# Counting products of a routing step: float32r operands in place of bfloat16

## Chip, cores and metric

One Trainium2 chip, one of its cores. The metric is the device time of one execution in microseconds (us): three runs of the kernel before gave 1186.3, 1187.3 and 1188.73 us, median 1187.3 us.

## What is computed

Three layers in a row, all with float32 inputs and a float32 output: an attention with normalised queries and keys (4 batches, 12 heads, 448 positions, head size 64), an MLP from 768 to 2048 and back to 768 with a hard-swish between, and a layer of 8 experts. The last assigns each of the 1792 tokens to one expert, and every expert takes at most 224 tokens:

```python
logits = x @ w_gate                          # 1792 x 8
order = np.argsort(-logits.flatten())
for idx in order:
    tok, e = idx // E, idx % E
    if assigned[tok] >= 0 or counts[e] >= cap: continue
    assigned[tok] = e; counts[e] += 1
...
h = np.maximum(x[mask] @ w1[e], 0.0); out[mask] = h @ w2[e]
```

Pairs of token and expert are thus visited from the largest logit down; a token goes to the first expert that still has room.

## The kernel before

The program is one stream per engine. The large products run on TensorE in the type float32r: the operands are split into a high and a low float32r part, and three products (high by high, high by low, low by high) make one.

The attention and the first half of the MLP fill the first 650 us or so. From there to about 890 us TensorE computes the second half of the MLP, `y`, in a loop over tiles of 128 tokens (`passes`, lines 1151 to 1186). For each of 16 slices of the hidden width (`f`) the function `y_mm` (line 1110) is called for three products and two parts of the output, 512 columns (`hf` 0) and 256 columns (`hf` 1). So the products alternate, 512 columns, 256 columns, each with a stationary operand of 128 columns of `g2h` or `g2l`. These operands come by DMA (`gr`), are rounded on ScalarE (line 1053) and get their low part on GpSimd (line 1055).

The routing is done beside this. Its logits `L` are ready before. It is a generator, `routing()` (line 810), that does its work on VectorE and a few small products on TensorE, and yields a number: `y_mm` counts the products of `y`, and when that many have been issued it lets the generator go on (lines 1119 and 1120). The table `Y` (line 62) holds these numbers. They alone set where the routing's small products stand in TensorE's order.

Seven rounds (`r`, line 891) each find, for every expert, the limit above which its tokens are taken:

- `best()` (line 879) marks in `A` (128 partitions x 14 x 8, 0 or 1) the best expert that each token has left.
- Six steps search the threshold digit by digit, three on the high half of the logit's bits (`kh`), three on the low half (`kl`). A step compares all keys with 40 candidates at once, `C` (128 x 14 x 40, 0 or 1, line 917). Then 14 products on TensorE (line 922) count for each candidate and expert: the stationary operand is a slice of `C`, 128 x 40, the moving one a slice of `A`, 128 x 8. VectorE compares the counts with the room left, `G` (40 x 8, line 924). One more product (line 927), with `ones` (40 x 128) stationary, sums `G` over the 40 candidates onto all partitions. VectorE makes of it the next digit (`js`, `pre`, `thr`) and the next `C`.
- The step's yields are `Y[1]` = 11 products of `y` between `C` and its counts and `Y[2]` = 3 between the counts and the product with `ones`.
- At the end of a round three more products: `ones` by `rgb` (line 944), `ones` by `Tb` and `tri` by `Tb` (lines 965 and 966), with `ones` and `tri` 128 x 128 stationary and 14 or 16 moving columns.

After the rounds one product with `tri` (line 998) and 14 with `oh` (line 1017) give the table of tokens, `sidx`, from which the experts' inputs are gathered.

So there are 7 x 6 = 42 bursts of 14 counting products (588), 42 products with `ones` behind them, 7 x 3 at the ends of rounds, and one at line 998. All of these operands are bfloat16 before; `oh` and `mq` (line 1017) are bfloat16 before and after.

```python
if queue: ...
elif cnt[0] >= cnt[1]:                       # y_mm, line 1119
    cnt[1] = cnt[0] + next(route, 10 ** 9)
...
for c in range(NTC):                         # routing, line 921
    nc.tensor.matmul(n, C[:, c, :], A[:, c, :], start=(c == 0), stop=(c == NTC - 1))
```

Of the kernel before, what the change touches and what calls it, by code (L numbers as in the profile page):

```python
# [8 lines left out]
F32 = mybir.dt.float32  # L9
F32R = mybir.dt.float32r  # L10
BF16 = mybir.dt.bfloat16
# [10 lines left out]
def kernel(  # L22
# [14 lines left out]
    nc = tc.nc  # L37
    B, H, S, D = q.shape
    DM, FF = w_in.shape
    E = w_gate.shape[1]  # L40
# [8 lines left out]
    NTC = NT // 128  # L49
# [760 lines left out]
    def routing():  # L810
# [4 lines left out]
        JM = 40  # L815
        V = nc.vector

        def t_(shape, name, dt=F32, bufs=1):
            return rp.tile(shape, dt, name=name, bufs=bufs)

        def psum(p, n):
            return ps.tile([128, 512], F32, name="rt", tag="b", bufs=8)[:p, :n]

        tri = t_([128, 128], "tri", BF16)
        V.tensor_scalar(tri, jp[:, :128], 0.0, None, op0=OP.is_gt)
        ones = t_([128, 128], "ones", BF16)
        V.memset(ones, 1.0)
        ji = t_([128, JM], "ji", I32)
        nc.gpsimd.iota(ji, pattern=[[1, JM]], base=1, channel_multiplier=0)
        jt = {}  # L830
# [42 lines left out]
        def bc(x):  # L873
            return x[:, :, None].to_broadcast([128, NTC, E])

        def be(x):
            return x[:, None, :].to_broadcast([128, NTC, E])

        def best():
            m = t_([128, NTC], "m")  # L880
            V.tensor_reduce(m, Lw, axis=AX.X, op=OP.max)
            w = t_([128, NTC, E], "w")
            V.tensor_tensor(w, Lw, bc(m), op=OP.is_equal)
            V.tensor_tensor(w, w, be(e8), op=OP.mult)
            V.tensor_reduce(m, w, axis=AX.X, op=OP.max)
            A = t_([128, NTC, E], "A", BF16)
            V.tensor_tensor(A, w, bc(m), op=OP.is_equal)
            return A

        yield Y[0]  # L890
        for r in range(E - 1):
            A = best()
            w = t_([128, NTC, E], "w")
            kh = t_([128, NTC], "kh")
            kl = t_([128, NTC], "kl")
            V.tensor_tensor(w, A, hi, op=OP.mult)
            V.tensor_reduce(kh, w, axis=AX.X, op=OP.add)
            V.tensor_tensor(w, A, lo, op=OP.mult)
            V.tensor_reduce(kl, w, axis=AX.X, op=OP.add)
            V.tensor_tensor(kh, kh, U, op=OP.mult)  # L900
            found = []
            for key, (J, steps) in zip((kh, kl), DIG):
                if key is kl:
                    hs = found[0]
                    t = t_([128, NTC], "t16")
                    V.scalar_tensor_tensor(kl, kh, hs, kl, op0=OP.is_equal, op1=OP.mult)
                    V.tensor_scalar(t, kh, hs, 70000.0, op0=OP.is_gt, op1=OP.mult)
                    V.tensor_tensor(kl, kl, t, op=OP.add)
                p = t_([128, 1], "pre" + ("h" if key is kh else "l"))
                V.memset(p, 0.0)  # L910
                for i, x in enumerate(steps):
                    thr = jt[x][:, :J]
                    if i:
                        thr = t_([128, JM], "thr")[:, :J]
                        V.tensor_scalar(thr, jt[x][:, :J], p, None, op0=OP.add)
                    C = t_([128, NTC, JM], "C", BF16)[:, :, :J]
                    V.tensor_tensor(C, key[:, :, None].to_broadcast([128, NTC, J]),  # L917
                                    thr[:, None, :].to_broadcast([128, NTC, J]), op=OP.is_ge)
                    yield Y[1]
                    n = psum(J, E)  # L920
                    for c in range(NTC):
                        nc.tensor.matmul(n, C[:, c, :], A[:, c, :], start=(c == 0), stop=(c == NTC - 1))  # L922
                    G = t_([JM, E], "G", BF16)[:J]
                    V.tensor_tensor(G, n, cap[:J], op=OP.is_ge)
                    yield Y[2]
                    n = psum(128, E)
                    nc.tensor.matmul(n, ones[:J, :], G, start=True, stop=True)
                    js = t_([128, 1], "js")
                    V.tensor_reduce(js, n, axis=AX.X, op=OP.max)
                    V.scalar_tensor_tensor(p, js, float(x), p, op0=OP.mult, op1=OP.add)  # L930
                found.append(p)
            gt = t_([128, NTC], "gt")
            ge = t_([128, NTC], "ge")
            V.tensor_scalar(gt, kl, found[1], None, op0=OP.is_gt)
            V.tensor_scalar(ge, kl, found[1], None, op0=OP.is_ge)
            rg = t_([128, 2, E], "rg")
            for i, x in enumerate((gt, ge)):
                V.tensor_tensor(w, A, bc(x), op=OP.mult)
                V.tensor_reduce(rg[:, i], w.rearrange("p c e -> p e c"), axis=AX.X, op=OP.add)
            rgb = t_([128, 2, E], "rgb", BF16)  # L940
            V.tensor_copy(rgb, rg)
            yield Y[3]
            n = psum(128, 2 * E)
            nc.tensor.matmul(n, ones, rgb.rearrange("p a e -> p (a e)"), start=True, stop=True)
            es = t_([128, E], "es")
            m1 = t_([128, 1], "m1")
            V.tensor_tensor(es, n[:, E:], cap, op=OP.is_ge)
            V.tensor_tensor(es, es, e8, op=OP.mult)
            V.tensor_reduce(m1, es, axis=AX.X, op=OP.max)
            V.tensor_scalar(es, es, m1, None, op0=OP.is_equal)  # L950
            V.tensor_tensor(cap, cap, n[:, :E], op=OP.subtract)
            rem = t_([128, 1], "rem")
            t8 = t_([128, E], "t8")
            V.tensor_tensor(t8, es, cap, op=OP.mult)
            V.tensor_reduce(rem, t8, axis=AX.X, op=OP.add)
            V.tensor_tensor(w, A, be(es), op=OP.mult)
            T = t_([128, NTC], "T")
            V.tensor_reduce(T, w, axis=AX.X, op=OP.add)
            V.tensor_tensor(ge, ge, gt, op=OP.subtract)
            V.tensor_tensor(T, T, ge, op=OP.mult)  # L960
            Tb = t_([128, NTC], "Tb", BF16)
            V.tensor_copy(Tb, T)
            yield Y[4]
            n, n2 = psum(128, NTC), psum(128, NTC)
            nc.tensor.matmul(n2, ones, Tb, start=True, stop=True)
            nc.tensor.matmul(n, tri, Tb, start=True, stop=True)
            cc = t_([128, NTC, NTC], "cc")
            V.tensor_tensor(cc, ctri, n2[:, None, :].to_broadcast([128, NTC, NTC]), op=OP.mult)
            cum = t_([128, NTC], "cum")
            V.tensor_reduce(cum, cc, axis=AX.X, op=OP.add)  # L970
            V.scalar_tensor_tensor(cum, n, rem, cum, op0=OP.subtract, op1=OP.is_lt)
            V.tensor_tensor(T, T, cum, op=OP.mult)
            V.tensor_tensor(gt, gt, T, op=OP.add)
            V.tensor_tensor(U, U, gt, op=OP.subtract)
            V.tensor_tensor(w, A, bc(gt), op=OP.mult)
            V.tensor_tensor(asg, asg, w, op=OP.add)
            V.scalar_tensor_tensor(cap, es, 9999.0, cap, op0=OP.mult, op1=OP.add)
            V.scalar_tensor_tensor(Lw, be(es), -3.0e38, Lw, op0=OP.mult, op1=OP.add)
            yield Y[5]
        A = best()  # L980
        w = t_([128, NTC, E], "w")
        V.tensor_tensor(w, A, bc(U), op=OP.mult)
        V.tensor_tensor(asg, asg, w, op=OP.add)
# [5 lines left out]
        for d in (1, 2, 4, 8):  # L989
# [1 line left out]
            V.tensor_tensor(s2[:, d:], s[:, d:], s[:, :NTC - d], op=OP.add)  # L991
            V.tensor_copy(s2[:, :d], s[:, :d])
            s = s2
        tot = t_([128, E], "tot", BF16)
        V.tensor_copy(tot, s[:, NTC - 1])
        yield Y[6]
        n = psum(128, E)
# [17 lines left out]
        n = psum(CP, 4 * E)  # L1015
# [4 lines left out]
        V.scalar_tensor_tensor(sidx, n[:, :2 * E], 128.0, lo, op0=OP.mult, op1=OP.add)  # L1020

    route = routing()
    SEGS = []
    for t in range(NTC):
# [283 lines left out]
```

## Time and profile before

| what | before |
|---|---|
| median of three runs | 1187.3 us |
| the profiled execution's own time | 1187.51 us |
| its span, first to last instruction | 1185.7 us |
| busy: TensorE products (PE) | 1121.4 us, 95% of the span |
| busy: weight loads (PEld, beside PE) | 907.1 us, 76% |
| busy: VectorE (DVE) | 704.5 us, 59% |
| busy: ScalarE (ACT) | 520.7 us, 44% |
| busy: GpSimd (POOL) | 486.7 us, 41% |
| mean granted TensorE clock | 0.985 of 2.4 GHz |

The time around the span, 1.8 us, is that of start and end. A product shows in the trace as two records, the load of its stationary operand (LDWEIGHTS, PEld) and the product itself (MATMUL, PE). Products are pipelined: a record of a product reaches from its issue to its modelled end, and the next one begins long before that. What a product costs is therefore the distance from its start to the start of the next, and where a product's own load is late, its record begins with the load and is longer by it. In the trace all 4-byte products are called "f32", float32r ones too. A shape such as "128*40 128x8" is contracted rows * stationary columns, and the moving operand.

### The profile page before, as it was taken

The numbers are of one execution on the slowest core, as the hardware profiler recorded it, in microseconds if no ns is written. First come the engines' busy times: TensorE is split into PE (matmuls) and PEld (weight loads), VectorE is DVE, ScalarE is ACT, GpSimd is POOL, SyncE is SP. The second block draws the span as 40 slices with busy tenths as digits, with TensorE's granted clock in tenths as the row PEclk, the third lists the DMA queues.
The fourth block names the chain that finished last, engine by engine and source line by source line (L and its number), as shares of the span: only waits on it lengthen the run. The fifth ranks groups of instructions, "written<-read, shape, count | busy, mean of one in ns | idle before, by whom it ended". The sixth has DMA issues, their size and how long they took to land.

```text
span 1185.7 us, 19464 instructions
## 1 busy us (share of the span) xinstructions
PE 1121.4 (95%) x7204; PEld 907.1 (76%) x7204; DVE 704.5 (59%) x1467; ACT 520.7 (44%) x941; POOL 486.7 (41%) x363
## 2 busy tenths in 40 slices
PE   3888989999999999999999999999997999999997
PEld 2777756667667667787777777777877899999997
DVE  7887877776657744212341566666674756655550
ACT  3655655645545555543442111111123666665550
POOL 2321454664345433112444222222244677765550
PEclk9988999999999999999999999999999999999999
DMA  4465898977776896659986222222235898877731
GB/s 124 116 178 143 248 312 241 314 252 274 236 250 227 267 299 207 213 191 282 354 299 194 69 59 82 59 67 77 63 102 138 252 264 252 232 232 222 234 122 44
DMA packets 210706, 230.83 MB, mean 195 GB/s; under 512 B 24338, under 2 KB 183732, under 8 KB 210612
## 3 DMA queue, kind: packets, MB, share of 16 engines
q1 hardware_dynamic: 207284, 218.58, 59.8%
q0 software_dynamic: 3328, 11.01, 3.1%
q8 instruction: 56, 0.92, 0.3%
q14 instruction: 38, 0.31, 0.1%
HBM read 178.57 MB, written 50.98 MB: 194 GB/s over the span
## 4 chain that ended last, share of the span: by engine, by line
PE 67%; DVE 13%; DMA 8%; issue 5%; ACT 3%; POOL 3%; SPq 1%; POOLq 0%; DVEq 0%; ACTq 0%
PE y L1112 17%; PE h L522 15%; PE y L1260 8%; PE h L1196 5%; PE st L333 4%; PE av L422 3%; PE h L1198 3%; PE av L373 2%; PE sm L431 2%; DMA w<-cv 2%; PE rt L922 2%; DMA we_s<-in_moe_w_dram 1%; DVE C L917 1%; DMA w_hl<-w 1%; PE lg L564 1%
## 5 line engine op out<-in xcount | busy, mean ns | idle before, releaser
L522 PE MATMUL h<-xh,w 128*128 128x448 f32 x768 | 238.5, 380 | 0.8 <-DVE mx L314 0.4
L522 PEld LDWEIGHTS h<-xh,w 128*128 128x128 f32 x768 | 142.9, 190 | 34.8 <-issue 22.2
L1055 POOL TENSOR_TENSOR g2l<-gr,g2h 128x512 fp32r<-128x512 f32 x60 | 78.6, 1311 | 197.3 <-ACT g2h L1053 161.9
L522 PE MATMUL h<-xl,w 128*128 128x448 f32 x384 | 145.4, 379 | 0.0
L314 DVE TENSOR_REDUCE mx<-s 112x1 f32<-112x448 f32 x192 | 105.7, 612 | 51.6 <-PE s L311 51.5
L1053 ACT ACTIVATE g2h<-gr 128x512 fp32r<-128x512 f32 x60 | 37.9, 631 | 222.1 <-PE y L1112 163.9
L1112 PE MATMUL y<-woh,g2l 128*128 128x512 f32 (+1 forms) x448 | 127.8, 347 | 1.0 <-POOL g2l L1055 1.0
L1112 PE MATMUL y<-woh,g2h 128*128 128x512 f32 (+1 forms) x448 | 127.1, 347 | 0.0
L1112 PE MATMUL y<-wol,g2h 128*128 128x512 f32 (+1 forms) x448 | 125.8, 345 | 0.0
L118 POOL TENSOR_TENSOR wel<-we_s,weh 128x768 fp32r<-128x768 f32 x48 | 97.8, 2042 | 40.3 <-ACT weh L117 28.9
L117 ACT ACTIVATE weh<-we_s 128x768 fp32r<-128x768 f32 x107 | 88.4, 841 | 54.1 <-DMA we_s<-in_moe_w_dram 35.8
L118 DVE TENSOR_TENSOR wel<-we_s,weh 128x768 fp32r<-128x768 f32 x59 | 80.0, 1365 | 54.0 <-ACT weh L117 53.8
L344 ACT ACTIVATE ph<-st 112x448 f32<-112x448 f32 x192 | 93.0, 544 | 41.9 <-PE st L333 41.0
L415 POOL TENSOR_TENSOR pa<-ph 112x448 f32<-112x448 f32 x68 | 84.7, 1265 | 47.9 <-ACT ph L344 47.9
L1196 PE MATMUL h<-xe,weh 128*128 128x448 f32 x318 | 101.0, 377 | 1.1 <-DVE xe L1147 1.1
L522 PEld LDWEIGHTS h<-xl,w 128*128 128x128 f32 x384 | 73.1, 190 | 11.4 <-issue 7.1
L1112 PEld LDWEIGHTS y<-woh,g2h 128*128 128x128 f32 x448 | 71.9, 189 | 11.7 <-issue 2.3
L1112 PEld LDWEIGHTS y<-woh,g2l 128*128 128x128 f32 x448 | 72.1, 188 | 10.9 <-POOL g2l L1055 1.3
L1112 PEld LDWEIGHTS y<-wol,g2h 128*128 128x128 f32 x448 | 71.7, 188 | 9.9 <-issue 0.7
L1198 PE MATMUL h<-xe,wel 128*128 128x224 f32 x318 | 76.5, 268 | 0.0
L525 ACT ACTIVATE r<-h,half 128x448 f32<-128x448 f32 x64 | 40.7, 635 | 74.3 <-PE h L522 61.4
L1260 PE MATMUL y<-weh,hh 128*112 128x384 f32 x216 | 73.1, 338 | 0.0
(242 smaller groups left out, 2326.2 us busy)
## 6 DMA issues: line engine op xcount, KB each, us to landing
we_s<-in_moe_w_dram SPq DMA_DIRECT2D x128, 384.0 KB, 3.9
w<-w_hl SPq DMA_DIRECT2D x32, 768.0 KB, 5.7
gr<-g_dr SPq DMA_DIRECT2D x52, 256.0 KB, 2.9
wraw<-in_moe_w_in_dram SPq DMA_DIRECT2D x16, 768.0 KB, 6.8
win_v<-w SPq DMA_DIRECT2D x32, 384.0 KB, 8.2
w_hl<-w SPq DMA_DIRECT2D x16, 768.0 KB, 6.0
wraw<-in_moe_w_out_dram SPq DMA_DIRECT2D x16, 768.0 KB, 5.3
g_dr<-g SPq DMA_DIRECT2D x48, 224.0 KB, 5.0
```

The source lines that it names most:

```text
L117: nc.scalar.activation(hi, raw, AF.Copy)
L118: eng.tensor_tensor(lo, raw, hi.bitcast(F32), op=OP.subtract)
L314: mx = nc.vector.tensor_reduce(MX[i][:, s, c:c + 1], pp[s][:CP, :S], axis=AX.X, op=OP.max)
L333: nc.tensor.matmul(pp[s][:CP, :S], a[r], b[r], start=(n == 0), stop=(n == len(todo) - 1))
L344: nc.scalar.activation(e, pp[s][:CP, :S], AF.Exp)
L415: nc.gpsimd.tensor_tensor(PA[i, s, n], PP[i, s, 2 * n][0], PP[i, s, 2 * n + 1][0], op=OP.add)
L522: nc.tensor.matmul(p[:, :S], lhs[:, c], x[:, c], start=(n == 0), stop=(n == 3 * NC - 1))
L1055: eng.tensor_tensor(gl, g, gh.bitcast(F32), op=OP.subtract)
L1112: nc.tensor.matmul(pp[hf][:, :COLS[hf].stop - COLS[hf].start], a[:, f % QF], w[:, COLS[hf]], start=(f == 0 and n == 0), stop=(f == NF - 1 ...
L1196: mm = [lambda: nc.tensor.matmul(p[:, :4 * CP], wh[:, fo], x.rearrange("d k t -> d (k t)"), start=(c == 0), stop=(c == NC - 1), skip_group ...
L1198: lambda: nc.tensor.matmul(p[:, :2 * CP], wl[:, fo], x[:, 0], start=False, stop=False, skip_group_check=True)]
L1260: nc.tensor.matmul(p[:CP, :HW], a[:, f, tk], w[:, o], start=(f == 0 and n == 0), stop=(f == FB - 1 and n == 2))
```

## The change

All operands of the routing's products but `oh` and `mq` become float32r: `tri`, `ones`, `A`, `C`, `G`, `rgb`, `Tb` and `tot`. VectorE reads `A` through a float32 view. Shapes, counts, the table `Y` and the rest of the program are the same.

```diff
-        tri = t_([128, 128], "tri", BF16)
+        tri = t_([128, 128], "tri", F32R)
         V.tensor_scalar(tri, jp[:, :128], 0.0, None, op0=OP.is_gt)
-        ones = t_([128, 128], "ones", BF16)
-        V.memset(ones, 1.0)
+        ones = t_([128, 128], "ones", F32R)
+        V.memset(ones.bitcast(F32), 1.0)
...
-            A = t_([128, NTC, E], "A", BF16)
+            A = t_([128, NTC, E], "A", F32R)
             V.tensor_tensor(A, w, bc(m), op=OP.is_equal)
-            return A
+            return A, A.bitcast(F32)
...
-            A = best()
+            AR, A = best()
...
-                    C = t_([128, NTC, JM], "C", BF16)[:, :, :J]
+                    C = t_([128, NTC, JM], "C", F32R)[:, :, :J]
...
-                        nc.tensor.matmul(n, C[:, c, :], A[:, c, :], start=(c == 0), stop=(c == NTC - 1))
-                    G = t_([JM, E], "G", BF16)[:J]
+                        nc.tensor.matmul(n, C[:, c, :], AR[:, c, :], start=(c == 0), stop=(c == NTC - 1))
+                    G = t_([JM, E], "G", F32R)[:J]
...
-            rgb = t_([128, 2, E], "rgb", BF16)
+            rgb = t_([128, 2, E], "rgb", F32R)
...
-            Tb = t_([128, NTC], "Tb", BF16)
+            Tb = t_([128, NTC], "Tb", F32R)
...
-        A = best()
+        A = best()[1]
...
-        tot = t_([128, E], "tot", BF16)
+        tot = t_([128, E], "tot", F32R)
```

No instruction of VectorE, ScalarE, GpSimd or the DMA queues changes its place. On TensorE a bfloat16 product is written as two instructions, a load and a product, a float32r one as a single instruction that holds its load. Around the first burst and the product with `ones` behind it, TensorE's order before ends so (the last two counting products, three products of `y`, the load and the product with `ones`, the next of `y`):

```order
L922 LDWEIGHTS C
L922 MATMUL rt<-A,C 40x8
L1112 MATMUL y<-woh,g2h 128x256
L1112 MATMUL y<-wol,g2h 128x512
L1112 MATMUL y<-wol,g2h 128x256
L927 LDWEIGHTS ones
L927 MATMUL rt<-G,ones 128x8 [waits DVE_49]
L1112 MATMUL y<-woh,g2l 128x512 [waits Pool_49]
```

The load of `ones` waits for nothing there; only its product waits for `G`. With the change the same place is:

```order
L922 MATMUL rt<-A,C 40x8 [waits DVE_49]
L922 MATMUL rt<-A,C 40x8 x13
L1112 MATMUL y<-woh,g2h 128x256
L1112 MATMUL y<-wol,g2h 128x512
L1112 MATMUL y<-wol,g2h 128x256
L927 MATMUL rt<-G,ones 128x8 [waits DVE_49]
L1112 MATMUL y<-woh,g2l 128x512 [waits Pool_49]
```

The products stand where they stood; the wait for `G` now holds the load as well. At the end of a round, the same for `Tb`; before:

```order
L965 LDWEIGHTS ones
L965 MATMUL rt<-Tb,ones 128x14 [waits DVE_49]
L966 LDWEIGHTS tri
L966 MATMUL rt<-Tb,tri 128x14
```

and with the change:

```order
L965 MATMUL rt<-Tb,ones 128x14 [waits DVE_49]
L966 MATMUL rt<-Tb,tri 128x14
```

Here too the load of `ones` comes behind the wait.

## Rows read from the trace of the kernel before

**Rows 1.** Busy time by engine, 650 to 890 us: PE, PEld, DVE, ACT, POOL.

```profile
650.00:890.00 240.00, 234.25 (x1719) 186.31 (x1717) 156.83 (x536) 35.83 (x60) 63.40 (x49) 1.00 0.26 73
```

**Rows 2.** Chain that ended last, 650 to 690 us, shares by line.

```profile
by line: PE y L1112 82.6%; PE rt L922 8.7%; DVE C L917 4.7%; PE rt L927 1.9%; DVE thr L915 0.6%; DVE js L929 0.4%; DVE prel L930 0.4%; PE rt L965 0.4%; issue 0.4%; PE rt L944 0.3%; PE rt L966 0.1%
```

**Rows 3.** Timeline, PE, 653.8 to 658.2 us: start, length, engine, line, count, idle before.

```profile
653.85 0.40 PE L1112 MATMUL y<-woh,g2h 128*128 128x512 f32 x1
654.18 0.51 PE L922 MATMUL rt<-A,C 128*40 128x8 bf16 x14
654.62 0.38 PE L1112 MATMUL y<-woh,g2h 128*128 128x256 f32 x1
...
655.29 0.18 PE L927 MATMUL rt<-G,ones 40*128 40x8 bf16 x1
655.39 0.61 PE L1112 MATMUL y<-woh,g2l 128*128 128x512 f32 x2
```

**Rows 4.** Timeline, weight loads (PEld), the same stretch.

```profile
654.18 0.42 PEld L922 LDWEIGHTS <-C 128*40 128x40 bf16 x14 [0.25 <-issue]
...
655.28 0.09 PEld L927 LDWEIGHTS <-ones 40*128 40x128 bf16 x1 [0.25 <-issue]
```

**Rows 5.** Groups by shape: busy us, mean ns of one, idle before.

```profile
L1112 PE MATMUL y<-woh,g2h 128*128 128x256 f32 x224 | 64.5, 288 | 0.0
L922 PE MATMUL rt<-A,C 128*40 128x8 bf16 x588 | 21.4, 167 | 3.3 <-DVE C L917 3.1
L927 PEld LDWEIGHTS <-ones 40*128 40x128 bf16 x42 | 3.9, 92 | 10.7 <-issue 10.7
```

**Rows 6.** Timeline, 888.9 to 890.4 us: the bfloat16 products with oh.

```profile
888.77 0.39 PE L1112 MATMUL y<-woh,g2h 128*128 128x512 f32 x1
...
889.00 0.98 PEld L1017 LDWEIGHTS <-oh 128*112 128x112 bf16 x14
889.23 0.85 PE L1017 MATMUL rt<-mq,oh 128*112 128x32 bf16 x14
```

**Rows 7.** Timeline, 301.4 to 302.6 us: float32r, from 64 rows to 128.

```profile
301.50 0.45 PE L311 MATMUL s<-kh,qh 64*112 64x448 f32 x1 [0.34 <-DVE g L527]
...
301.88 0.19 PEld L522 LDWEIGHTS h<-xl,w 128*128 128x128 f32 x1 [0.21 <-issue]
```

**Rows 8.** Timeline at 40.0 us, and the tile av: 4-byte products with few moving columns.

```profile
39.77 1.05 PE L373 MATMUL av<-vv,ph 112*112 112x66 f32 x9
...
L373 PE MATMUL av<-vv,ph x448: 221/262/452, 36.5 to 524.9; 112*112 112x66 f32 x150
```

**Rows 9.** Timeline, 665.3 to 668.9 us: a step in which C is late.

```profile
666.35 1.28 POOL L1055 TENSOR_TENSOR g2l<-gr,g2h 128x512 fp32r<-128x512 f32 x1 [4.53 <-ACT g2h L1053]
666.38 1.85 DVE L917 TENSOR_TENSOR C<-kl,thr 128x560 bf16<-128x560 f32 x1
...
668.28 0.42 PEld L922 LDWEIGHTS <-C 128*40 128x40 bf16 x14 [0.76 <-DVE C L917]
```

**Rows 10.** Waits, PE, 650 to 890 us: total, times, longest.

```profile
PE rt L922 <- DVE C L917: 3.1, 7, 0.4
```

**Rows 11.** Timeline at 676 us and 679 us: the products that end a round.

```profile
675.70 0.17 DVE L941 CAST rgb<-rg 128x16 bf16<-128x16 f32 x1
...
675.93 0.17 PE L944 MATMUL rt<-rgb,ones 128*128 128x16 bf16 x1
...
679.05 0.17 DVE L962 CAST Tb<-T 128x14 bf16<-128x14 f32 x1
...
679.27 0.17 PE L965 MATMUL rt<-Tb,ones 128*128 128x14 bf16 x1
...
679.30 0.17 PE L966 MATMUL rt<-Tb,tri 128*128 128x14 bf16 x1
```

**Rows 12.** VectorE on 112 elements: bfloat16 written, and float32 written.

```profile
L887 DVE TENSOR_TENSOR A<-w,m x8: 270/277/1008, 648.9 to 879.9; 128x112 bf16<-128x112 f32 x8
...
L883 DVE TENSOR_TENSOR w<-Lw,m 128x112 f32<-128x112 f32 x8 | 2.2, 270 | 0.1
```

## Prediction
> **What bounds the kernel now.** I read the busy times by engine first. In the stretch in which the routing runs, 650 to 890 us, TensorE is busy for 234.25 of 240 us at full clock, VectorE for 156.83, ScalarE and GpSimd for far less [rows 1]. The chain of waits says the same: from 650 to 690 us 82.6% of it are products of `y`, 8.7% the counting products and 1.9% those with `ones`, all on TensorE; VectorE's `C` has 4.7% [rows 2]. So what the routing's small products take out of TensorE's time is paid in full, except in the steps where TensorE waits for VectorE. The waits give those: seven times, once in a round, the counting products wait for `C`, 3.1 us together [rows 10].
>
> Then I read the timeline of one step, the products [rows 3] and the loads [rows 4]. The reader should see how much stands around the small products:
>
> - Ahead of the counting products TensorE pauses. The product of 512 columns starts at 653.85; 512 columns at 2.4 GHz are 0.21 us; yet the first load of `C` starts at 654.18, 0.12 after that.
> - The counting products follow each other every 25 ns: 14 loads in 0.42 us, 14 products in 0.51, of which the last one's own length is 0.167 [rows 5], so (0.51 - 0.17) / 13.
> - Behind them there is a pause again. The last one starts at 654.18 + 0.51 - 0.17 = 654.52, the next load of `y` at 654.62, and that product's record is 0.38 long instead of 0.29 [rows 5]: about 0.10 of it is its own load of 128 columns, which nothing hides.
> - The product with `ones` has the same pauses of 0.1 on both sides (655.29 to 655.39 behind it), but its own load of 128 columns costs 0.01: load at 655.28, product at 655.29.
>
> Is the pause due to the type or to the shape? Rows from other places tell. The products with `oh` are bfloat16 too, with 112 columns: their first load starts together with the product of `y` ahead of it, at 889.00, and the first product takes its natural slot at 889.23, 0.23 after it, as 888.77 to 889.00 is [rows 6]. So bfloat16 among float32r does not pause. A float32r product that contracts 64 rows does: it starts at 301.50 with its load of 0.07 to 0.09 in front, has 448 columns (0.19 us), and the load of the 128-row product behind starts only at 301.88 [rows 7]. The pause belongs to a change of the array's shape, 40 columns or 40 rows against 128.
>
> **The change, part by part.** The order of the instructions stays; what changes is the load of a stationary operand, the pauses, and what a wait holds.
>
> *VectorE: nothing.* Writing 112 elements as bfloat16 takes 270 ns, as float32 270 ns [rows 12]; the engine's rows are the same in number and place.
>
> *Pace of the 588 counting products.* No row shows a float32r load of 40 columns. Bounds: not under the 25 ns of now, since the same columns are read at twice the bytes. For the upper side, the nearest rows at equal columns are 112 columns: bfloat16, `oh`, (0.85 - 0.20) / 13 = 50 ns [rows 6]; 4-byte, line 373, whose 66 moving columns leave the load to set the pace, (1.05 - 0.26) / 8 = 99 ns [rows 8]. Scaling 25 by 99/50 gives 50 ns. I take 40 ns, an estimate from three of these rows: bfloat16 from 40 to 112 columns goes from 25 to 50 ns, 0.35 ns a column and 11 fixed; twice 0.35 for 4 bytes gives 39 at 40 columns (and 89 at 112, where 99 was measured). Each nanosecond counts 42 x 13 = 546 times, 0.55 us.
>
> *Pauses around the counting products.* They stay at most (as with every narrow shape in the rows), or go. I take that they go: in the changed program as built these products address the full width of the array, though they fill 40 columns; the bfloat16 ones address half of it. A shape that doesn't change has no reason to pause [rows 6]. The Trainium skill, page "PSUM — Partial Sum Buffer", section "The four PSUM rules", says that float32r matmuls force the full column group; no row here shows a narrow float32r product. By that rule the sum is the one below; without it, the one of the second rival.
>
> So a burst costs, from the 512-column product ahead to the next of `y`: before 653.85 to 654.62 + 0.09, that is 0.86 us. With the change 0.23 for the slot [rows 6], 13 x 0.040 = 0.52, and 0.10 for the bare load of `y`: 0.85. In 35 bursts -0.01 each, -0.35 us. In the seven that wait for `C` the pause ahead was hidden in the wait, so only the one behind goes: 0.20 more for the pace, 0.02 more for the first load, 0.09 less: +0.13, together +0.9 us.
>
> *The 42 products with ones.* Their 40 rows are still a change of shape, so the pauses stay. The load of 128 columns now costs what the bare load of `y` costs, 0.10 in place of 0.01. Its wait for `G` is met long before: `G` follows the burst, three products of `y` ahead. +0.09 to 0.10 each. In the seven steps where `C` waits for GpSimd it costs nothing: `C` starts at 666.38, just behind GpSimd's `g2l` at 666.35, takes 1.85 us and ends 0.6 after it [rows 9], so a `C` that is ready to start 0.1 later still ends there. 35 x 0.10 = +3.5 us. [...]
>
> *Ends of rounds.* `rgb` is ready at 675.87 and its product starts at 675.93; `Tb` at 679.22, product at 679.27 [rows 11]. These products wait for VectorE with their loads done. Now the load comes behind the wait: +0.10 for `rgb`, +0.10 for `Tb`, and the load of `tri` takes 0.10 where the two products were 0.03 apart [rows 11]: +0.07. Per round 0.27, in seven 1.9 us, with line 998 2.0 us. Below: nothing, if they are ready earlier in other rounds.
>
> **Sum:** -0.35 + 0.9 + 3.5 + 2.0 = +6.0 us. The profiled execution took 1187.5 us (span 1185.7), so 1193.5; the median of the runs lies 0.2 lower: **1193.3 us**. No cover is lost elsewhere: ScalarE, GpSimd and the DMAs of this stretch are paced by the products of `y`, and get more time.
>
> **Rivals.**
>
> 1. *Not slower:* the 4-byte loads of 40 columns are not paced by their bytes. If 25 ns is a floor of load and product under which both types fall, the counting products stay at 25 ns and the lost pauses are a clear gain: 15 x 0.55 = 8.2 us less, total -2.2, 1185.1 us. For it: from 112 to 40 columns the bfloat16 pace falls less than the columns do, 50 to 25 ns, so a part of the 25 is no load and may cover a longer one. Against: 99 ns for 112 columns leave 35 at 40 columns in proportion. It decides below 29 ns (zero at 40 - 6.0/0.55).
> 2. *The pauses stay* also around the float32r counting products, as around every product of 64 or fewer columns in the trace. Then a burst costs 0.22 more than my sum says (0.13 ahead with the bare first load, 0.09 behind), 35 x 0.22 + 7 x 0.09 = +8.3: 1201.6 us.
> 3. *Faster:* besides rival 1 the collisions of `C` with GpSimd shift apart, since steps get longer and shorter by a tenth of a microsecond and `C` starts only 0.03 behind `g2l` [rows 9]; up to 3.1 us of waits go [rows 10], to 1182. The same mechanism can add waits, about 0.5 x 7 us to my sum: 1196.8.
> 4. *The change does nothing:* not possible in the loads of `ones`; the program holds other instructions.
>
> **How the numbers follow.** My forecast 0.58 (pace 32 to 50 ns: 1189 to 1199 us); rival 1 0.18; rival 2 0.15; rival 3, the fast side, 0.07; anything else 0.02, slower. 0.2% of the time, 2.4 us, is about what a measurement of this kernel can tell. Faster by more: 0.08, rival 3 and the lowest end of 1. Within: 0.17, the rest of 1. Slower: 0.75. The range 1186.0 to 1202.0 holds my forecast, rival 2 and the upper half of rival 1. Alone, the forecast's range is 1189 to 1199.
>
> **What would show it.** Right: loads of `C` that start with the product of `y` ahead, and no idle before them; 14 counting products in about 0.17 + 13 x 0.04 = 0.69 us; the load of `ones` 0.19 long instead of 0.09 and its product's record about 0.1 longer; no change in VectorE's rows but the type. Wrong: a distance between counting products near 25 or above 50 ns; "idle, issue" of 0.25 still ahead of each burst; a change in the seven waits for `C`; or another time outside 650 to 890 us.

## Result and the profile after

| what | before | after |
|---|---|---|
| median of 20 runs each | 1187.74 us | 1194.46 us |
| ratio of the runs, with its 95% interval | 1 | 1.0059 [1.0046, 1.0072] |
| profiled span | 1185.7 us | 1191.2 us |
| mean granted clock | 0.985 | 0.983 |

The change makes the kernel slower by 0.59%: 0.0059 x 1187.7 = 7.0 us, by the interval 5.5 to 8.6. The forecast was 6.0 more. Of the 5.5 us between the two spans, 5.0 lie between the first and the last counting product. The rows of the tile `rt` show it (count; least, median and longest ns; first and last start). Before:

```profile
L922 PE MATMUL rt<-A,C x588: 166/166/183, 654.2 to 864.6; 128*40 128x8 bf16 x196
```

After:

```profile
L922 PE MATMUL rt<-A,C x588: 167/179/200, 655.3 to 870.7; 128*40 128x8 f32 x196
L927 PEld LDWEIGHTS rt<-G,ones x42: 182/183/183, 656.5 to 871.5; 40*128 40x128 f32 x42
```

210.4 us became 215.4. Below I call this distance the **stretch**. It is taken from one profiled execution of each kernel, and is a sharper measure than the time: span less stretch varies over the twelve profiled kernels of this study between 971 and 979 us, though little of what they change lies there (the last product with `ones`, the end of the seventh round and line 998).

In the windows, TensorE is as full as before, 234.72 of 240 us against 234.25 [rows 1], and the loads have grown from 186 to 193; the granted clock (the column behind the five engines) is 1.00 of 2.4 GHz in both, so no part of the difference in this stretch is the clock's:

```profile
650.00:890.00 240.00, 234.72 (x1689) 193.00 (x1687) 152.77 (x530) 36.33 (x60) 63.42 (x49) 1.00 0.26 73
```

The timeline of the same first step, PE, that answers to [rows 3]:

```profile
655.07 0.40 PE L1112 MATMUL y<-woh,g2h 128*128 128x512 f32 x1
655.31 0.67 PE L922 MATMUL rt<-A,C 128*40 128x8 f32 x14
655.83 0.36 PE L1112 MATMUL y<-woh,g2h 128*128 128x256 f32 x1
...
656.48 0.27 PE L927 MATMUL rt<-G,ones 40*128 40x8 f32 x1
656.68 0.61 PE L1112 MATMUL y<-woh,g2l 128*128 128x512 f32 x2
```

and the loads, as in [rows 4]:

```profile
655.07 0.81 PEld L922 LDWEIGHTS rt<-A,C 128*40 128x40 f32 x14
655.80 0.20 PEld L1112 LDWEIGHTS y<-woh,g2h 128*128 128x128 f32 x1
...
656.48 0.18 PEld L927 LDWEIGHTS rt<-G,ones 40*128 40x128 f32 x1 [0.25 <-DVE G L924]
```

The reader should see three things. The first load of `C` starts with the product of `y` ahead, at 655.07, and no idle stands before it; the first counting product takes its natural slot, 0.24 behind. The counting products follow each other every (0.67 - 0.18) / 13 = 38 ns, and the load of `y` starts right where the last of them does, at 655.80. And from the product with `ones` to the next of `y` it is now 0.20, where it was 0.10; the idle of 0.25 ahead of its load is still there, by the profile with another name.

The waits of PE, 650 to 890 us, as in [rows 10] (total, times, longest), where `Tb` had 1.5 us in its one wait before, in the last round:

```profile
PE rt L922 <- DVE C L917: 3.0, 7, 0.5
PE rt L965 <- DVE Tb L962: 0.3, 1, 0.3
```

The seven waits for `C` are the same, because `C` still starts just behind GpSimd's `g2l`, as in [rows 9]; from the timeline:

```profile
667.78 1.28 POOL L1055 TENSOR_TENSOR g2l<-gr,g2h 128x512 fp32r<-128x512 f32 x1 [4.63 <-PE y L1112]
667.81 1.86 DVE L917 TENSOR_TENSOR C<-kl,thr 128x560 fp32r<-128x560 f32 x1
```

At the first end of a round, as in [rows 11]:

```profile
677.26 0.17 DVE L941 CAST rgb<-rg 128x16 fp32r<-128x16 f32 x1
677.49 0.28 PE L944 MATMUL rt<-rgb,ones 128*128 128x16 f32 x1
677.63 0.59 PE L1112 MATMUL y<-woh,g2h 128*128 128x512 f32 x2
...
680.96 0.28 PE L965 MATMUL rt<-Tb,ones 128*128 128x14 f32 x1
681.09 0.26 PE L966 MATMUL rt<-Tb,tri 128*128 128x14 f32 x1
681.20 0.36 PE L1112 MATMUL y<-woh,g2l 128*128 128x256 f32 x1
```

Before, the products of `y` behind line 944 and line 966 began so:

```profile
675.96 0.59 PE L1112 MATMUL y<-woh,g2h 128*128 128x512 f32 x2
...
679.33 0.37 PE L1112 MATMUL y<-woh,g2l 128*128 128x256 f32 x1
```

From line 944 to `y` it takes 0.14 in place of 0.03, from line 965 to 966 0.13 in place of 0.03, and from there to `y` 0.11 in place of 0.03.

Added over the starts of all 42 steps in the two timelines, the 4.9 us from the first burst to behind the last product with `ones` divide so: bursts with the three products of `y` behind them +0.3; products with `ones` +3.9 (0.09 in every step); the six ends of rounds between +0.9; all other products of `y` -0.2.

### The profile page after: what moved, and what is told of

The parts are those of the page before. It is cut to its first block, busy times and chain, and to the rows that moved or that the text cites. A ratio compares the mean times of both kernels' runs of the same rounds, so it can differ in the third digit from the quotient of the medians.

```text
span 1191.2 us, 19471 instructions
## 1 busy us (share of the span) xinstructions
PE 1127.7 (95%) x7204; PEld 918.5 (77%) x7204; DVE 702.6 (59%) x1467; ACT 519.9 (44%) x941; POOL 489.6 (41%) x363
## 4 chain that ended last, share of the span: by engine, by line
PE 67%; DVE 14%; DMA 6%; issue 5%; ACT 3%; POOL 2%; SPq 1%; POOLq 0%; DVEq 0%; ACTq 0%
PE y L1112 15%; PE h L522 14%; PE y L1260 8%; PE h L1196 6%; PE st L333 4%; PE av L422 3%; PE h L1198 3%; PE av L373 2%; PE rt L922 2%; PE sm L431 2%; DVE mx L314 1%; DVE cv L142 1%; DVE C L917 1%; PE lg L564 1%; DMA gr<-g_dr 1%
```

## Experiments

Each kernel is named after its edit. Three asked which part of the change costs what, six what makes the pauses and what the pace, and the last puts two shapes together.

### Counting products alone

```diff
-            A = t_([128, NTC, E], "A", BF16)
+            A = t_([128, NTC, E], "A", F32R)
...
-                    C = t_([128, NTC, JM], "C", BF16)[:, :, :J]
+                    C = t_([128, NTC, JM], "C", F32R)[:, :, :J]
```

> The kernel before with A and C alone as float32r; ones, tri, G, rgb, Tb and tot stay bfloat16. Theory (the counting products' pauses of 0.1 us on either side go and are paid back by the pace, 38 ns in place of 25; the loss lies in the products with ones): 35 bursts of -0.01 and seven of +0.13, +0.5 us over the kernel before, which is within 0.2%; in the trace no idle before the loads of C, 14 products in 0.67 us, the load of ones still 0.09 long. Rival (the counting products themselves carry the loss, the products with ones next to nothing): +4 to +6 us, and a burst that costs 0.1 us more from the product of 512 columns ahead to the next of y.

Ratio 1.0014 [0.9996, 1.0033], +1.7 us between -0.5 and +3.9. The tile's row has the stretch at 211.2, 0.8 more than before:

```profile
L922 PE MATMUL rt<-A,C x588: 167/179/200, 653.5 to 864.7; 128*40 128x8 f32 x196
```

The step without a wait takes 3.39 us (before 3.40). The rival would need 4 us: it falls.

### The products with ones and the ends of rounds alone

```diff
-        tri = t_([128, 128], "tri", BF16)
+        tri = t_([128, 128], "tri", F32R)
...
-        ones = t_([128, 128], "ones", BF16)
+        ones = t_([128, 128], "ones", F32R)
...
-                    G = t_([JM, E], "G", BF16)[:J]
+                    G = t_([JM, E], "G", F32R)[:J]
```

and the same for `rgb`, `Tb` and `tot`.

> The kernel before with ones, tri, G, rgb, Tb and tot as float32r; C and A stay bfloat16. Theory: 35 products with ones at +0.10 us (their load of 128 columns takes 0.18 in place of 0.09 and nothing hides it) and seven ends of rounds at +0.27, together +5.5 us; bursts of counting products as before, with idle of 0.25 ahead of them and 25 ns between products. Rival (the loss lies in the counting products): within 1 us of the kernel before, although the loads of ones are longer, since they would be hidden beside the product of y ahead.

Ratio 1.0036 [1.0020, 1.0052], +4.3 us (2.4 to 6.2). The tile's row puts the stretch at 214.8, +4.4, and the timeline shows the old burst with the new product with `ones`, 0.20 ahead of `y`:

```profile
L922 PE MATMUL rt<-A,C x588: 165/166/184, 655.4 to 870.2; 128*40 128x8 bf16 x196
```

```profile
753.63 0.51 PE L922 MATMUL rt<-A,C 128*40 128x8 bf16 x14
754.07 0.38 PE L1112 MATMUL y<-woh,g2h 128*128 128x256 f32 x1
...
754.74 0.27 PE L927 MATMUL rt<-G,ones 40*128 40x8 f32 x1
754.94 0.61 PE L1112 MATMUL y<-woh,g2l 128*128 128x512 f32 x2
```

So the loss lies here, 1 us under the 5.5 expected. The two parts add up: 0.8 + 4.4 = 5.2 against 5.0 for the whole change.

### The ends of rounds alone

```diff
+        onesr = t_([128, 128], "onesr", F32R)
+        V.memset(onesr.bitcast(F32), 1.0)
...
-            nc.tensor.matmul(n, ones, rgb.rearrange("p a e -> p (a e)"), start=True, stop=True)
+            nc.tensor.matmul(n, onesr, rgb.rearrange("p a e -> p (a e)"), start=True, stop=True)
```

and so on for `Tb`, `tri` and `tot`.

> The kernel before, with float32r only in the products at the ends of rounds and the one behind the last round: tri, rgb, Tb, tot and a second ones of float32r for them; counting products, G and its ones bfloat16. It asks how large the third term of the prediction is. The prediction's 0.27 a round: the stretch from the first to the last burst becomes 6 x 0.27 = 1.6 us longer, 211.7 in place of 210.1. What the two kernels with float32r ones suggest, 0.11 to 0.20 a round: 0.7 to 1.2 us longer. Rival (nothing, since VectorE's next step is ready earlier than TensorE asks for it): 210.1 again. The time itself, 1 to 2 us more, is too little for one look.

The tile's row:

```profile
L924 PE MATMUL rt<-A,C x588: 165/166/184, 652.7 to 864.9; 128*40 128x8 bf16 x196
```

A single run took 1187.9 us. The stretch by this row is 212.2, 1.8 more than before; by the products of `y` ahead of the first and the last burst, which the expectation goes by, 211.8 against 210.1, and each of the six ends takes 0.27 more. By itself the term has the predicted size; the smaller figures and the rival fall.

### Counting products with 128 bfloat16 columns

```diff
+        Cw = t_([128, NTC * JM + CW - JM], "C", BF16)
...
-                        nc.tensor.matmul(n, C[:, c, :], A[:, c, :], start=(c == 0), stop=(c == NTC - 1))
+                        nc.tensor.matmul(n, Cw[:, c * JM:c * JM + CW], A[:, c, :], start=(c == 0), stop=(c == NTC - 1))
```

`CW` is 128; `n` has 128 rows, of which 40 are read.

> The kernel before, bfloat16 throughout, but each counting product loads 128 columns of C (40 that count and 88 more that are not used, the next slices and zeros). Theory (shape): with 128 columns the shape never changes, so the idle behind the burst goes (0.09 each), while ahead of it the load, which needs all of the array's columns at once and is not begun beside the product of y, still costs about what the pause did; pace 25 ns, since 128 bfloat16 columns load as fast as 40; about 35 x 0.09 = 3 us less than the kernel before. Rival (the pauses belong to bfloat16 among float32r, not to the shape): both pauses stay and the time is within 1 us of the kernel before. Rival 2 (the pace follows the columns): 25 ns becomes 50 ns or more, 546 x 0.025 = 14 us more.

Ratio 0.9961 [0.9942, 0.9980], -4.6 us (-6.9 to -2.4), where 3 less were expected; the stretch 204.1, 6.3 less, by the tile's row:

```profile
L925 PE MATMUL rt<-A,C x588: 165/166/181, 654.1 to 858.2; 128*128 128x8 bf16 x196
```

In the timeline (PE and PEld) a burst looks like this:

```profile
750.46 0.39 PE L1115 MATMUL y<-wol,g2h 128*128 128x512 f32 x1
750.69 0.51 PE L925 MATMUL rt<-A,C 128*128 128x8 bf16 x14
...
750.69 0.42 PEld L925 LDWEIGHTS <-C 128*128 128x128 bf16 x14 [0.16 <-issue]
751.06 0.36 PE L1115 MATMUL y<-wol,g2h 128*128 128x256 f32 x1
```

bfloat16 throughout, and both pauses are gone: both rivals fall. Half of the theory fell as well. The load is indeed not begun beside the product ahead (0.16 idle), but it costs nothing: load and product stand at 750.69 together, in the natural slot. The pace is 26 ns at 128 columns as at 40.

### Counting products with 80 columns, in either type

```diff
-        CW = 128
+        CW = 80
```

This is the last kernel's edit with another width, in the kernel before, and then, with `Cw` in float32r, in the changed kernel.

> The kernel before with bfloat16 counting products that load 80 columns of C, 40 of them unused. Theory (the pauses belong to a width of 64 columns or fewer against 128): the idle ahead of the loads of C and behind the burst goes although the operands stay bfloat16; the pace follows the columns without the fast load that 128 get, about 39 ns between products (from 25 ns at 40 columns and 50 at 112); burst about 13 x 0.014 - 0.19, as before within 0.05 us, time within 2 us of the kernel before. Rival 1 (only a load of all 128 columns takes the pauses away): pauses of 0.1 on both sides stay and the kernel is 5 to 8 us slower than before. Rival 2 (pace 25 ns at 80 columns as at 40 and 128): as with 128 columns, 6 us less than before.

> The changed kernel, but each counting product loads 80 columns of C (40 that count, and the next slice's or zeros, not used). Theory (the pace of the float32r counting products is set by the columns that are loaded, 0.83 ns a column and some 5 fixed): about 72 ns between products in place of 38, 546 x 0.034 = 18 to 19 us more than the changed kernel. Rival (38 ns is a floor of issuing a load and a product): pace and time as in the changed kernel.

The bfloat16 kernel, timeline (PE and PEld):

```profile
656.26 0.40 PE L1115 MATMUL y<-wol,g2h 128*128 128x512 f32 x1
656.27 0.81 PEld L925 LDWEIGHTS <-C 128*80 128x80 bf16 x14
656.50 0.67 PE L925 MATMUL rt<-A,C 128*80 128x8 bf16 x14
657.03 0.36 PE L1115 MATMUL y<-wol,g2h 128*128 128x256 f32 x1
```

The float32r kernel, its row in the tile `rt` and the timeline of a burst (PE):

```profile
L925 PE MATMUL rt<-A,C x588: 167/213/275, 648.8 to 885.8; 128*80 128x8 f32 x196
```

```profile
656.28 0.39 PE L1115 MATMUL y<-woh,g2l 128*128 128x512 f32 x1
656.51 1.10 PE L925 MATMUL rt<-A,C 128*80 128x8 f32 x14
657.47 0.36 PE L1115 MATMUL y<-woh,g2l 128*128 128x256 f32 x1
```

The bfloat16 burst of 80 columns is the float32r burst of 40, row for row: no idle, 0.81 of loads that start with the product ahead, 38 ns. A single run took 1186.6 us beside 1185.8 before. Of the float32r one the rows give (1.10 - 0.21) / 13 = 68 ns on the mean; the first distance is short, and the others are the 72 ns that were expected. A single run took 1210.2 us; its stretch, 648.8 to 885.8 in the tile's row, is 21.6 longer than the changed kernel's, of which the burst, 0.43 longer, makes 42 x 0.43 = 18 (the rest was not followed up). So the pauses go at 80 columns in bfloat16 too, and the pace follows the bytes of the load: equal at 40 x 4 and 80 x 2 bytes a row, 68 at 80 x 4. At 80 bfloat16 columns the slower pace takes back what the pauses gave.

### The product with ones on 128 rows, in the changed kernel

```diff
+        G = t_([128, E], "G", F32R)
+        V.memset(G.bitcast(F32), 0.0)
...
-                    nc.tensor.matmul(n, ones[:J, :], G, start=True, stop=True)
+                    nc.tensor.matmul(n, ones, G, start=True, stop=True)
```

> The changed kernel, but the products with ones contract 128 rows in place of 40: G has 128 rows, of which 88 are zero, and ones is used whole. Theory (a pause of 0.1 us on either side belongs to a change of the array's shape, here from 128 rows to 40 and back, and a load of the full shape is begun beside the product of y ahead): the two pauses go and the bare load is hidden, 0.28 us less in each of 35 steps, 10 us less than the changed kernel, about 1184; the load of ones starts at the start of the product of y ahead, or when G comes. Rival 1 (the 0.1 us is the cost of reading 128 float32r columns whatever the shape): within 1 us of the changed kernel. Rival 2 (the load begins early but then waits for G, which comes three products of y after the burst): 3 to 6 us less only, with waits for G of 0.05 to 0.2 us in the trace.

Ratio to the kernel before 0.9920 [0.9902, 0.9938], 1177.2 us; against the changed kernel 0.9920 / 1.0059, 1.4% less, some 16 us. The timeline (PE and PEld):

```profile
755.10 0.19 PEld L928 LDWEIGHTS rt<-G,ones 128*128 128x128 f32 x1
755.21 0.17 PE L928 MATMUL rt<-G,ones 128*128 128x8 f32 x1
755.24 0.59 PE L1113 MATMUL y<-woh,g2l 128*128 128x512 f32 x2
```

The float32r load of 128 columns is now begun 0.11 ahead, beside the product of `y`, and `y` follows after 0.03 in place of 0.20. Both rivals fall; a step takes 3.16 us, 0.31 less than the changed kernel's 3.47. That makes the 10 us of the theory. The rest comes from the seven late steps, 4.09 in the changed kernel and 3.16 to 3.19 here, 0.6 more than the others gain: TensorE no longer waits for `C` there. `C` took up to 1.86 us in the changed kernel (667.81 above); its row here, with the timeline of the step in which it was late:

```profile
L919 DVE TENSOR_TENSOR C<-kl,thr x14: 741/743/744, 664.1 to 851.6; 128x560 fp32r<-128x560 f32 x14
```

```profile
664.07 0.74 DVE L919 TENSOR_TENSOR C<-kl,thr 128x560 fp32r<-128x560 f32 x1
664.12 1.83 POOL L1056 TENSOR_TENSOR g2l<-gr,g2h 128x512 fp32r<-128x512 f32 x1 [4.23 <-ACT g2h L1054]
```

`C` starts 0.05 ahead of `g2l` where it started 0.03 behind, and now it is GpSimd that takes 1.83, off the path.

### Full shapes, bfloat16 throughout, and 72 rows

The kernel with 128 bfloat16 columns, and in it

```diff
+        G = t_([128, E], "G", BF16)
+        V.memset(G, 0.0)
...
-                    nc.tensor.matmul(n, ones[:J, :], G, start=True, stop=True)
+                    nc.tensor.matmul(n, ones, G, start=True, stop=True)
```

The second kernel has `ones[:72, :]` and `G[:72]` there.

> The kernel before in bfloat16 throughout, with full shapes: loads of 128 columns of C, and ones used whole with G on 128 rows, 88 of them zero. Theory (the shape makes the pauses, and a bfloat16 load of 128 columns costs 0.01 to 0.02 us when nothing covers it): the same as with float32r ones on 128 rows, within 2 us, 1171 to 1176 when the kernel before takes 1186, about 0.03 us between the product with ones and the next of y in place of 0.106. Rival (only float32r products run without a pause beside float32r ones): the product with ones keeps 0.1 us on both sides, and the time is that of the kernel with 128 bfloat16 columns alone, about 1181.

> The bfloat16 kernel with full shapes, but ones and G on 72 rows in place of 128. Theory (the pauses go with 64 rows or fewer, and 72 already address all rows): as with 128 rows, about 0.04 us from the product with ones to the next of y, a step of 3.0 us, time 1165 to 1172. Rival (anything but 128 rows pauses): 0.1 us on both sides of it again, as with 40 rows, 0.16 more in each of 35 steps, some 6 us more.

Full shapes: ratio 0.9846 [0.9822, 0.9870], median 1168.8 us beside 1185.8; step 3.01 us, stretch 192.7, by the tile's row:

```profile
L927 PE MATMUL rt<-A,C x588: 165/166/180, 657.2 to 849.9; 128*128 128x8 bf16 x196
```

The product with `ones` in the timeline (PE and PEld):

```profile
658.15 0.10 PEld L931 LDWEIGHTS <-ones 128*128 128x128 bf16 x1 [0.16 <-issue]
658.16 0.18 PE L931 MATMUL rt<-G,ones 128*128 128x8 bf16 x1
658.20 0.59 PE L1116 MATMUL y<-woh,g2l 128*128 128x512 f32 x2
```

With 72 rows a single run took 1171.2 us; the stretch is 192.4, and in the timeline `y` again comes 0.04 behind:

```profile
752.82 0.18 PE L931 MATMUL rt<-G,ones 72*128 72x8 bf16 x1
752.86 0.59 PE L1116 MATMUL y<-woh,g2l 128*128 128x512 f32 x2
```

Both theories of the pauses hold, both rivals fall; the time with full shapes lies 2 us below the 1171 to 1176 that were expected. The shape makes the pause, not the type.

### 128 bfloat16 columns of C, float32r ones on 128 rows

```diff
+        onesr = t_([128, 128], "onesr", F32R)
+        G = t_([128, E], "G", F32R)
...
-                    nc.tensor.matmul(n, ones[:J, :], G, start=True, stop=True)
+                    nc.tensor.matmul(n, onesr, G, start=True, stop=True)
```

also in the kernel with 128 bfloat16 columns.

> Full shapes for both: C bfloat16 with loads of 128 columns, G and a second ones in float32r on 128 rows, the ends of rounds bfloat16 as before. Theory (what the two separate kernels gained adds up): a burst 0.18 us less than before, a product with ones 0.17 less, 35 x 0.35 = 12 us, and where C no longer meets GpSimd's transfers up to 3 more: 1171 to 1175 when the kernel before takes 1186. Rival (gains do not add, since C or G come too late and TensorE waits instead): not under 1177, with waits for C or G of 0.2 us and more per step.

Ratio 0.9855 [0.9834, 0.9877], median 1167.8 us beside 1185.8; stretch 192.4, from 654.2 to 846.6. The rival falls. The gain is 17 us where 12 to 15 were expected: 28 steps fall from 3.40 to 3.01 (0.39 in place of 0.35, 11 us) and the seven late ones from 3.93 to 3.01 (0.92, 6 us). It equals the kernel with bfloat16 alone. Both are faster than the kernel before and the changed one, and neither needs the change.

## Why the prediction was right

Median 1193.3 was forecast, 1194.46 came. In the stretch the terms forecast add up to 5.65 us (without the seventh end and line 998), and the traces have 5.0. That the total is so near is in part luck: the products with `ones` came out 0.4 larger, bursts and ends of rounds together 0.95 smaller. Step by step:

- **Pauses around the counting products.** They go, as taken; the rival in which they stay falls with the rows at 655.07 and 655.80. The reason given, a change of the array's shape, is shown from both sides: bfloat16 with 80 or 128 columns doesn't pause; on 40 rows both types pause, on 128 rows neither, on 72 bfloat16 doesn't. That float32r at 40 columns addresses the full width is not seen by itself; the missing pause agrees with it. The Trainium skill, page "TensorEngine Tiling (Array Packing)", section "Key Properties", says that changing the tiling mode drains the engine; the trace agrees in so far as it has a pause of 0.1 us at each change, and shows no more of what happens in it.
- **Pace.** 40 ns taken, 38 measured. The estimate came out near by another line than the rows have: from 80 and 112 bfloat16 columns (38 and 50 ns) it is 0.38 ns a column, which would give 23 at 40 columns, and 26 is measured at 40 and at 128 columns alike. So there is a floor by these rows, as rival 1 has it, but float32r loads of 40 columns lie above it; the rival needed 29 ns. The reason, that the load's bytes count, holds; that 40 is so near 38 is luck, since the line was drawn through that floor.
- **Bursts.** Forecast -0.35 + 0.9 = +0.55, measured +0.3. The counting products alone had no measurable effect on the time.
- **Products with ones.** +3.5 forecast, +3.9 measured: 0.09 in each of 42 steps. Here the forecast had 0.10 in 35 steps and nothing in the seven late ones, and that nothing was wrong: the wait doesn't absorb the 0.09, since `g2l`, which holds `C` up, starts 0.76 behind the product of `y` that follows the one with `ones`, before and after, and so comes later with it. The late steps grow by 0.16 in all, where 0.13 were forecast. The Trainium skill, page "TensorE: Matmul & The Clock Gate", section "Weight-path perf modes — Fast Weight Load (FWL) and DoubleRow", says that the fast weight load is on where 128 columns are loaded and the type is not FP32. The trace agrees: 128 bfloat16 columns load at a pace of 26 ns, 80 of them, fewer, at 38; the float32r record of 128 is 183 ns against 92.
- **Ends of rounds.** +2.0 forecast for seven and line 998; alone, 0.27 in each of six ends was measured, as forecast, but in the whole change 0.15, and 0.20 with float32r `ones` alone. With the bursts it is the term that came out smaller. The timelines show where most of it went. The three products cost 0.30 more in either kernel, but in the whole change the wait ahead of line 944 is gone: from the product of `y` ahead to it, 0.22 on the mean of six rounds before and 0.20 with the ends alone, 0.13 now. VectorE's `prel` (line 930), behind the last product with `ones` of a round, ends 0.01 to 0.02 behind GpSimd's `g2l` in all seven rounds, before:

```profile
672.65 1.28 POOL L1055 TENSOR_TENSOR g2l<-gr,g2h 128x512 fp32r<-128x512 f32 x1 [5.02 <-PE y L1112]
673.22 0.73 DVE L930 SCALAR_TENSOR_TENSOR prel<-js,prel 128x1 f32<-128x1 f32 x1
```

and after:

```profile
674.22 1.28 POOL L1055 TENSOR_TENSOR g2l<-gr,g2h 128x512 fp32r<-128x512 f32 x1 [5.15 <-PE y L1112]
674.87 0.65 DVE L930 SCALAR_TENSOR_TENSOR prel<-js,prel 128x1 f32<-128x1 f32 x1
```

Here `g2l` starts ahead of the product with `ones`, so the longer load of `ones` delays the products of `y` but not `prel` and `rgb`, and TensorE finds `rgb` ready. This is the cover that the prediction looked for in the late steps; it stands at the ends of rounds. The rest of the difference, some 0.05 a round, stays open.
- **Seven waits for C.** 3.1 forecast to stay, 3.0 measured. Rival 3 did not come in, since `C` and `g2l` kept their order and their distance of 0.03. A longer load of `ones` delays the product and the `y` behind it alike, so it can't part them. With 128 rows the pause *ahead* of the product goes: product, digit and `C` move 0.08 forward against `g2l`, and the order turns. The mechanism of that rival is real, and its point of decision lies a few hundredths of a microsecond away.

Behind the stretch the sum has the seventh end and line 998, 0.4 us. The traces don't show them as a loss: from the last counting product to the one of line 998 it takes 19.9 us before and 19.3 after, with 0.9 us less of waiting for `Tb` and `tot` (1.5 and 0.8 before, 0.3 and 1.1 after), and 20.1 with the ends alone. The prediction took from the waits only those for `C`. Why these became shorter was not isolated. Outside the stretch the span grew by 0.5 us in all, less than what the kernels scatter by there. The runs differ by 7.0 us (interval from 5.5), the two profiled spans by 5.5; what the rest is, no trace shows.

## What to carry to other kernels

Before changing a type for the sake of small products in a stream of large ones, look at what shape of the array they use: a product of 40 rows in either type, or of 40 columns in bfloat16, paid 0.1 us on each side among full ones, and padding to 72 rows or 80 columns took that away. The padding must not make the load slower: at 80 bfloat16 columns nothing was gained, at 128 columns, with `ones` on 128 rows, 1.5%. A type change moves two terms in opposite directions, the pauses (by the shape that the type brings) and the load (by its bytes, with 128 bfloat16 columns as cheap as 40), so price them apart, in the timeline, from the start of one large product to the start of the next.

## What was not expected of the hardware

- A bfloat16 load of 128 columns is not begun beside the product ahead, and still costs nothing (750.69), while bfloat16 loads of 80 and 112 columns are begun early (656.27, [rows 6]). Loading 128 columns where 40 are needed was free; loading 80 cost 12 ns more a product.
- VectorE's `C` and GpSimd's `g2l` don't share: whichever starts first runs at its own length (0.74 or 1.28 us), and the other takes 1.83 to 1.86. A lead of 0.05 in place of a lag of 0.03 was worth 0.5 to 0.6 us in each of seven steps. `prel` behind `g2l`, 0.53 to 0.73 long where it is 0.16 in other steps, shows the same.
